# Weight sums placed behind the feed-forward's splits, k and v loads behind the sums: an attention and feed-forward kernel

## Chip, cores and metric

One core of one Trainium2 chip. The metric is device microseconds of one execution; the time of a kernel is the median of its runs.

## What is computed

For each batch b and head h, k and v are averaged over groups of 8 of their 576 positions, the softmax of q against the 72 pooled keys weighs the 72 pooled values, and the result, 4608 rows of 512, goes through a feed-forward with a leaky relu:

```python
k_p = k.reshape(B, H, Sp, pool, D).mean(axis=3)
v_p = v.reshape(B, H, Sp, pool, D).mean(axis=3)
scores = scale * np.matmul(q, k_p.transpose(0, 1, 3, 2))
...
out = np.matmul(attn, v_p)
...
h = x @ w_in                  # 4608x512 @ 512x2048
g = np.maximum(0.01 * h, h)
return g @ w_out              # 4608x2048 @ 2048x512
```

q, k and v have the shape 8 x 8 x 576 x 64, all float32.

## The kernel before

Every large product is made of three fp32r matmuls: an operand is split into a high part (a cast) and a low part (operand less high part), and high x high, high x low and low x high are added in PSUM.

**The feed-forward** goes in runs over chunks of 512 rows (`CH`). The list `runs` numbers them from 0: runs 0 to 4 share chunks 0 and 1 with the start, runs 5 to 9 take chunks 2 to 6 in full, runs 10 and 11 the last two chunks. In runs 5 to 9 a run has 16 steps f. In step f, `m1` makes a 128 x 512 block of x @ w_in in the PSUM tile `ph` (twelve matmuls, L1141 to L1143); ACT applies Prelu in place (L1146) and casts `gh` (L1149), DVE subtracts `gl` (L1150). `m2`, two steps behind, multiplies `gh` and `gl` with w_out into four accumulators `acc` (twelve matmuls, L1327 to L1329). There are two `ph` buffers, so the m1 of step f+2 waits for the `gl` of step f. The last step of a run stores the four accumulators (L1363 ff.): half copied by ACT, half by DVE into a tile `o`, then a store on SP's queue.

**Runs 10 and 11** take the weight blocks in eight pairs (`PAIRS`) and multiply by sums and differences of a pair's four halves, so that a pair needs fewer matmuls (`pair`, L1233 ff.). These are made beforehand: `prepare(j)` (L1171 ff.) adds the high and low parts of two weight blocks on DVE (L1180), forms four sums and differences (L1182 to L1186), casts the two results to `wsumh` on ACT (L1189), subtracts on DVE (L1190) and stores them in DRAM (`kept`, four stores on SP, L1200). For the first four pairs (`OPEN`) a fifth store keeps the half A22 of the weights as it is. The work of `prepare` is cut in eight pieces and two pairs (`EACH`) belong to each of runs 5 to 8.

**The attention** of batches 2 to 7 runs beside these runs, in units that the loop at L1488 ff. hands out between the pieces of m1 and m2: `lk` and `lv` load and pool k and v of a batch (loads L287, L304, L317; adds on POOL L264 and L271), `ku` and `vu` form kT and the value tiles `v_hi`, `v_lo`, `v_rem` (`v_parts`, L521, is the scaled remainder of v), `qT` is q transposed (L564), then for each tile t of 128 rows and each half g of the heads `pss` (scores, L599), `e` and `red` (softmax, L607 to L640), `at` (scaled weights, POOL, L643 and L649), `rows` (a store of `at` to DRAM, L660), `blocks` (loaded back in another order, L669), `pp` (transposed by DVE, L680), `pT` (its split, L702 to L709) and `pa` (weights x values on PE, L724 to L727), whose result, split again, is x of the feed-forward.

**Buffers.** One tag, `raw`, with two buffers in turn, holds the parts of k and v as loaded (k0raw, k1raw, kremraw, v0raw, v1raw, vremraw of a batch, in this order) and the weight sums (`wsum`, `wsumh`). Whoever takes a buffer waits until all readers of what was in it are done. Outputs `o` have a tag of their own with three buffers.

**What sets the order.** PE's order is that of the program. The other engines' are set by a list scheduler, which places an instruction by its program position and by what it expects of the engines; each engine and each DMA queue then runs its list strictly in turn. `tc.issue_after(x)` puts the instructions under it behind x. In the program the pieces of `prepare` are spread over the first half of a run:

```python
while n > REST and formed < min(1, 2 * beat / beats) * PIECES_OF * EACH:
    formed += 1
    next(forming, None)
```

(a run has 64 beats), and `lk`, `lv` of the next batch are put in the middle of the run's units (L1498 to L1500).

Of the kernel before, what the change touches and what calls it, by code (L numbers as in the profile page):

```python
# [24 lines left out]
def tile_pooled_attention_ffn(  # L25
# [9 lines left out]
    nc = tc.nc  # L35
# [463 lines left out]
    def place_v(b, sums, rem):  # L499
        if b < 2:  # L500
            pvm = bank(b, f"pvm{b}").rearrange("a p x -> a (p x)")[:, : NK * D]
            for g, half in enumerate(sums):
                for i in range(2):
                    nc.tensor.matmul(
                        pvm[:, 2 * g * D : 2 * (g + 1) * D],
                        addup[:, 1 - i : 3 - i, :].rearrange("r i s -> r (i s)"),
                        half[:, i::2, :], start=i == 0, stop=i == 1,
                    )
            sums = pvm.rearrange("a (p d) -> a p d", p=NK)
        for i in range(2):  # L510
            r = slice(64 * i, 64 * i + 64)
            pin(nc.scalar.mul(v_hi[r, :, i, :], sums[r], 1.0 / POOL))
        for i in range(2):
            r = slice(64 * i, 64 * i + 64)
            pin(nc.vector.scalar_tensor_tensor(
                v_lo[r, :, i, :], sums[r], 1.0 / POOL, v_hi[r, :, i, :].bitcast(F32),
                op0=ALU.mult, op1=ALU.subtract,
            ))
        if b > 1:
            yield  # L520
            pin(nc.scalar.mul(v_parts, rem, 1.0 / POOL))  # L521
            yield
            pin(nc.vector.scalar_tensor_tensor(
                rem, rem, 1.0 / POOL, v_parts.bitcast(F32), op0=ALU.mult, op1=ALU.subtract
            ))
            nc.vector.tensor_scalar(rem, rem, signs[:, 1:2], None, op0=ALU.mult)
            nc.vector.scalar_tensor_tensor(
                rem, v_parts.bitcast(F32), signs[:, 0:1], rem, op0=ALU.mult, op1=ALU.add
            )
            nc.vector.tensor_tensor(  # L530
                v_rem, rem.unsqueeze(2).broadcast_to([P, 2, 4, D]),
                heads.unsqueeze(1).unsqueeze(3).broadcast_to([P, 2, 4, D]), op=ALU.mult,
            )
            return
        for g in range(2):
            r, lo = slice(32 * g, 32 * g + 32), slice(64 + 32 * g, 96 + 32 * g)
            nc.scalar.mul(v_parts[r, g], rem[r, 0], 1.0 / POOL)
            nc.vector.scalar_tensor_tensor(
                v_parts[lo, g], rem[r, 0], 1.0 / POOL, v_parts[r, g].bitcast(F32),
                op0=ALU.mult, op1=ALU.subtract,  # L540
            )
        pv = bank(b, f"pv{b}").rearrange("a p x -> a (p x)")[:, : 2 * D]
        nc.tensor.matmul(
            pv, spread, v_parts.rearrange("s g d -> s (g d)"), start=True, stop=True
        )
        nc.vector.tensor_tensor(
            v_rem, pv.rearrange("s (g d) -> s g d", g=2).unsqueeze(2).broadcast_to([P, 2, 4, D]),
            heads.unsqueeze(1).unsqueeze(3).broadcast_to([P, 2, 4, D]), op=ALU.mult,
        )
# [574 lines left out]
    parts = [(n, c, f) for n, (c, fs, _) in enumerate(runs) for f in fs]  # L1124
    partial = dram.tile([CH, DM], F32, name="partial")
    back = []
    gs, accs = {}, {}

    def m1(k):

        n, c, f = parts[k]
        xh, xl = x_parts(c)
        w = ws[0, f]
        ts = runs[n][2]
        r = slice(ts[0] * P, (ts[-1] + 1) * P)
        w_ = len(ts) * P
        nm = f"{n}_{f}"
        ph = ps_h.tile([P, CH], F32, tag="h", name=f"ph{nm}")[:, :w_]
        for kk in range(NK):
            ks = slice(kk * P, (kk + 1) * P)  # L1140
            nc.tensor.matmul(ph, w[:, 0, ks], xh[kk][:, r], start=kk == 0, stop=False)  # L1141
            nc.tensor.matmul(ph, w[:, 0, ks], xl[kk][:, r], start=False, stop=False)  # L1142
            nc.tensor.matmul(ph, w[:, 1, ks], xh[kk][:, r], start=False, stop=kk == NK - 1)  # L1143
            if kk == 1:
                yield
        nc.scalar.activation(ph, ph, AF.Prelu, alpha=0.01)  # L1146
        gh = three.tile([P, CH], F32R, tag="gh", name=f"gh{nm}")[:, :w_]
        gl = three.tile([P, CH], F32R, tag="gl", name=f"gl{nm}")[:, :w_]
        casts.append(nc.scalar.copy(gh, ph))  # L1149
        nc.vector.tensor_tensor(gl, ph, gh.bitcast(F32), op=ALU.subtract)  # L1150
        gs[k] = gh, gl
        yield

# [16 lines left out]
    def prepare(j):  # L1170

        f0, f1 = PAIRS[j]
        raw = two.tile([P, 2, DM], F32, tag="raw", name=f"wsum{j}")
        w = [raw[:, k, :] for k in range(2)]
        raw = two.tile([P, 2, DM], F32R, tag="raw", name=f"wsumh{j}")
        h = [raw[:, k, :] for k in range(2)]
        (a11, a12), (a21, a22) = ((x[:, :HALF], x[:, HALF:]) for x in w)
        for x, f in zip(w, (f0, f1)):
            whole = ws[0, f].bitcast(F32)
            nc.vector.tensor_tensor(x, whole[:, 0, :], whole[:, 1, :], op=ALU.add)  # L1180
            yield
        nc.vector.tensor_tensor(a22, a21, a22, op=ALU.add)  # L1182
        nc.vector.tensor_tensor(a21, a11, a21, op=ALU.subtract)
        yield
        nc.vector.tensor_tensor(a11, a22, a11, op=ALU.subtract)
        nc.vector.tensor_tensor(a12, a12, a11, op=ALU.subtract)  # L1186
        yield
        for x, y in zip(w, h):
            nc.scalar.copy(y, x)  # L1189
            nc.vector.tensor_tensor(x.bitcast(F32R), x, y.bitcast(F32), op=ALU.subtract)  # L1190
            yield
        ship = [
            (kept[j, :, 2 - 2 * i : 4 - 2 * i, k, :], part.rearrange("p (s x) -> p s x", s=2))
            for i in range(2) for k, part in enumerate((h[i].bitcast(F32), w[i]))
        ]
        if j < OPEN:
            ship.append((kept[j, :, 4], ws[0, f1].bitcast(F32)[:, :, HALF:]))
        yield
        for to, of in ship:
            nc.sync.dma_start(to, of)  # L1200
        yield

    seats = {}
# [139 lines left out]
    def store(n, c, t, a):  # L1343
        end = n == len(runs) - 1
        if end and t == NT - 1:

            r = 2 * S - 2 * TAIL + (c - 2) * CH + t * P
            for i, copy in enumerate((nc.scalar.copy, nc.vector.tensor_copy)):
                cols = slice(i * DM // 2, (i + 1) * DM // 2)
                o = two.tile([P, DM // 2], F32, tag="raw", name=f"o{n}_{t}{i}")  # L1350
                copy(o, a[:, cols])
                (nc.scalar if i == 0 else nc.sync).dma_start(out[r : r + P, cols], o)
            return

        pool, tag = (two, "raw") if n == REST - 1 and t > 1 else (five, "o")
        o = pool.tile([P, DM], F32, tag=tag, name=f"o{n}_{t}")
        if end:
            if t % 2:
                nc.scalar.copy(o, a)
            else:  # L1360
                nc.vector.tensor_copy(o, a)
        elif n == REST:
            nc.vector.tensor_tensor(o, a, back[t], op=ALU.add)  # L1363
        else:
            nc.scalar.copy(o[:, : DM // 2], a[:, : DM // 2])
            nc.vector.tensor_copy(o[:, DM // 2 :], a[:, DM // 2 :])
        if n == 0:
            nc.sync.dma_start(partial[t * P : (t + 1) * P, :], o)
        elif c < 2:
            nc.sync.dma_start(out[c * S + t * P : c * S + (t + 1) * P, :], o)  # L1370
        elif c == 2 and t == 0:
            for b in range(2):
                nc.sync.dma_start(out[b * S + CH : (b + 1) * S, :], o[TAIL * b : TAIL * (b + 1), :])
        else:
            r = 2 * S - 2 * TAIL + (c - 2) * CH + t * P
            nc.sync.dma_start(out[r : r + P, :], o)


    steps = []
# [100 lines left out]

    PIECES_OF = 8
    EACH = -(-len(PAIRS) // (FAST - 3))

    def sums_of(js):
        for j in js:
# [4 lines left out]
    for n, (c, fs, ts) in enumerate(runs[: REST + FAST - 1]):  # L1490
# [3 lines left out]
        if n >= REST:  # L1494
            nxt = n - REST + 2
            if nxt in waiting:
                us.insert(0, lambda nxt=nxt: carry(nxt))
            mid = len(us) // 2  # L1498
            for b in early[n]:
                us[mid:mid] = [att[b]["lk"], att[b]["lv"]]  # L1500
            if n == REST:
# [5 lines left out]
        for f in fs:  # L1507
# [23 lines left out]
            for slot in slots:  # L1531
                for _ in slot:
                    beat += 1
                    while done < min(len(us), len(us) * beat // (beats - behind)):
                        us[done]()
                        done += 1
                    while n > REST and formed < min(1, 2 * beat / beats) * PIECES_OF * EACH:
                        formed += 1
                        next(forming, None)
            at += 1  # L1540
        while done < len(us):
            us[done]()
# [80 lines left out]
```

## Time and profile before

| what | value |
|---|---|
| median of 3 runs | 923.64 us (922.68 to 926.41) |
| the profiled execution | 926.44 us |
| its span in the trace | 924.7 us |
| PE, DVE, ACT, POOL busy | 890.6, 499.3, 433.4, 211.2 us |
| mean granted clock of PE | 0.987 of full speed |
| HBM read, written | 76.94 MB, 30.54 MB |

The profiled execution lies 1.7 us over its own span and 2.8 us over the median of the runs. Times in the rows are counted from the start of the span. An engine's idle time is only named with the instruction that ended it and the releaser, in brackets.

### The profile page before, as it was taken

What the parts mean: (1) busy time and instruction counts of PE and PEld (TensorE: products, weight loads), DVE (VectorE), ACT (ScalarE), POOL (GpSimd) and SP (SyncE); (2) the same over time, 40 slices, a digit from 0 to 9 for tenths busy, and PEclk for the clock granted to TensorE, in tenths of its full rate; (3) what the DMA queues carried; (4) which work ended last, traced back from release to release, by engine and by line L of the source; (5) the groups of instructions that cost most, each with busy time, mean ns of one, the idle gap of its engine ahead of it and who ended that gap; (6) DMA issues with size and microseconds to landing.
All of it is one profiled execution on the core that took longest, in us unless ns stands there. A gap on an engine that the chain in (4) does not pass through costs nothing.

```text
span 924.7 us, 13658 instructions
## 1 busy us (share of the span) xinstructions
PE 890.6 (96%) x4587; PEld 761.1 (82%) x4587; DVE 499.3 (54%) x1178; ACT 433.4 (47%) x1354; POOL 211.2 (23%) x388
## 2 busy tenths in 40 slices
PE   4599999999999989999999999999999999999998
PEld 4478888788888868888888878888888889989997
DVE  6999569545384572636555555553455442452222
ACT  5788558344344443533444345342544344453332
POOL 4511110343423312411232122411210321010000
PEclk9799999999999989999999999999999999999999
DMA  9985231427346453423534343620532055414342
GB/s 259 303 262 166 66 72 46 97 58 188 111 130 171 107 162 86 113 47 120 154 82 96 87 137 102 138 62 25 148 81 63 0 164 160 122 47 137 105 135 80
DMA packets 153029, 108.37 MB, mean 117 GB/s; under 512 B 99840, under 2 KB 133376, under 8 KB 152960
## 3 DMA queue, kind: packets, MB, share of 16 engines
q1 hardware_dynamic: 144976, 90.86, 36.4%
q10 hardware_dynamic: 7984, 16.65, 6.4%
q8 instruction: 36, 0.59, 0.3%
q14 instruction: 33, 0.27, 0.1%
HBM read 76.94 MB, written 30.54 MB: 116 GB/s over the span
## 4 chain that ended last, share of the span: by engine, by line
PE 80%; DVE 7%; DMA 5%; POOL 2%; SPq 2%; ACT 2%; issue 1%; POOLq 0%; ACTq 0%; DVEq 0%
PE acc L1327 12%; PE acc L1328 12%; PE acc L1329 12%; PE ph L1141 9%; PE ph L1143 9%; PE ph L1142 9%; PE ends_y L1233 5%; PE ends_x L1233 3%; PE pss L599 3%; DMA q<-in_q_dram 1%; DMA blocks<-rows 1%; PE pa L725 1%; PE pa L727 1%; PE pa L726 1%; PE pa L724 1%
## 5 line engine op out<-in xcount | busy, mean ns | idle before, releaser
L1327 PE MATMUL acc<-w,gh 128*128 128x512 f32 x576 | 227.6, 395 | 0.0
L1328 PE MATMUL acc<-w,gh 128*128 128x512 f32 x576 | 225.2, 391 | 0.0
L1329 PE MATMUL acc<-w,gl 128*128 128x512 f32 x576 | 224.5, 390 | 0.0
L1141 PE MATMUL ph<-xh,w 128*128 128x512 f32 (+1 forms) x480 | 185.4, 386 | 3.6 <-DVE gl L1150 3.6
L1142 PE MATMUL ph<-xl,w 128*128 128x512 f32 (+1 forms) x480 | 181.9, 379 | 0.0
L1143 PE MATMUL ph<-xh,w 128*128 128x512 f32 (+1 forms) x480 | 181.9, 379 | 0.0
L1329 PEld LDWEIGHTS acc<-w,gl 128*128 128x128 f32 x576 | 108.2, 188 | 23.4
L1146 ACT ACTIVATE ph<-ph 128x512 f32<-128x512 f32 (+1 forms) x120 | 67.1, 559 | 127.0 <-PE ph L1143 126.3
L609 ACT ACTIVATE e<-pss,red 128x72 f32<-128x72 f32 (+1 forms) x320 | 97.6, 328 | 57.5 <-DVE red L607 57.2
L1327 PEld LDWEIGHTS acc<-w,gh 128*128 128x128 f32 x576 | 108.5, 188 | 19.2
L1328 PEld LDWEIGHTS acc<-w,gh 128*128 128x128 f32 x576 | 108.5, 188 | 18.6
L1150 DVE TENSOR_TENSOR gl<-ph,gh 128x512 fp32r<-128x512 f32 (+1 forms) x120 | 77.6, 648 | 74.7 <-ACT gh L1149 73.7
L1141 PEld LDWEIGHTS ph<-xh,w 128*128 128x128 f32 x480 | 91.5, 191 | 19.8 <-DVE gl L1150 4.2
L1143 PEld LDWEIGHTS ph<-xh,w 128*128 128x128 f32 x480 | 91.3, 190 | 16.9
L1142 PEld LDWEIGHTS ph<-xl,w 128*128 128x128 f32 x480 | 91.4, 190 | 15.4
L643 POOL TENSOR_TENSOR at<-e,red 128x128 f32<-128x128 f32 (+1 forms) x120 | 48.4, 423 | 193.1 <-DVE red L640 116.1
L1149 ACT CAST gh<-ph 128x512 fp32r<-128x512 f32 (+1 forms) x120 | 67.1, 559 | 3.1
L609 ACT ACTIVATION_READ_ACCUMULATOR e<-pss,red 128x1 f32 (+1 forms) x320 | 68.4, 214 | 0.0
L607 DVE TENSOR_REDUCE red<-pss 128x4 f32<-128x288 f32 (+1 forms) x80 | 35.9, 453 | 55.8 <-PE pss L599 53.1
L680 DVE STREAM_TRANSPOSE pp<-blocks 128x384 f32<-128x384 f32 (+1 forms) x60 | 44.4, 760 | 38.6 <-DMA blocks<-rows 38.5
L702 ACT CAST pT_hi<-pp 128x384 fp32r<-128x384 f32 (+1 forms) x80 | 36.4, 479 | 45.9 <-DVE pp L680 42.6
L599 PE MATMUL pss<-kT,qT 128*128 128x144 f32 x320 | 48.8, 294 | 3.8 <-DVE qT L564 1.1
(244 smaller groups left out, 1263.5 us busy)
## 6 DMA issues: line engine op xcount, KB each, us to landing
seat<-kept ACTq DMA_DIRECT2D x21, 512.0 KB
rows<-at SPq DMA_DIRECT2D x48, 192.0 KB
blocks<-rows SPq DMA_DIRECT2D x48, 192.0 KB
out_dram<-o SPq DMA_DIRECT2D x34, 256.0 KB
w_bits<-in_moe_w_in_dram SPq DMA_DIRECT2D x16, 512.0 KB
w_bits<-in_moe_w_out_dram SPq DMA_DIRECT2D x16, 512.0 KB
q<-in_q_dram SPq DMA_DIRECT2D x96, 64.0 KB
kept<-wsumh SPq DMA_DIRECT2D x16, 256.0 KB
```

The source lines that it names most:

```text
L599: nc.tensor.matmul(sc[:, 2 * SP * i : 2 * SP * (i + 1)], qT[:, p, :], kT[:, p, :, :].rearrange("d i s -> d (i s)"), start=True, stop=True,)
L609: ins = nc.scalar.activation(e[:n, h, :], scv[:n, h, :], AF.Exp, bias=mx[:n, h : h + 1], accum_out=sm[:n, h : h + 1],)
L1141: nc.tensor.matmul(ph, w[:, 0, ks], xh[kk][:, r], start=kk == 0, stop=False)
L1142: nc.tensor.matmul(ph, w[:, 0, ks], xl[kk][:, r], start=False, stop=False)
L1143: nc.tensor.matmul(ph, w[:, 1, ks], xh[kk][:, r], start=False, stop=kk == NK - 1)
L1146: nc.scalar.activation(ph, ph, AF.Prelu, alpha=0.01)
L1149: casts.append(nc.scalar.copy(gh, ph))
L1150: nc.vector.tensor_tensor(gl, ph, gh.bitcast(F32), op=ALU.subtract)
L1233: nc.tensor.matmul(out, w[:, stay, ks], move, start=start and i + n == 0, stop=i + n == 3, skip_group_check=True,)
L1327: nc.tensor.matmul(a, gh[:, r], hi, start=first, stop=False)
L1328: nc.tensor.matmul(a, gh[:, r], lo, start=False, stop=False)
L1329: nc.tensor.matmul(a, gl[:, r], hi, start=False, stop=last)
```

## The change

Five edits:

- Scaling `v_parts` on ACT is put behind the scaling of `v_hi`.
- The A22 stores (`kept[j, :, 4]`) are put behind the newest store of an output tile.
- The fourth output tile of run 9 takes a `raw` buffer instead of one of the output buffers.
- `lk` and `lv` come after two thirds of a run's units instead of a half, from run 5 on.
- The pieces of `prepare` are spread over beats 8 to 30 of the 64, and each is put behind the newest `gh` cast on ACT and the newest `gl` subtract on DVE.

```diff
-            pin(nc.scalar.mul(v_hi[r, :, i, :], sums[r], 1.0 / POOL))
+            ins = pin(nc.scalar.mul(v_hi[r, :, i, :], sums[r], 1.0 / POOL))
...
-            pin(nc.scalar.mul(v_parts, rem, 1.0 / POOL))
+            with tc.issue_after(ins.ins):
+                pin(nc.scalar.mul(v_parts, rem, 1.0 / POOL))
...
-    gs, accs = {}, {}
+    gs, accs, lows, sent = {}, {}, [], []
...
-        nc.vector.tensor_tensor(gl, ph, gh.bitcast(F32), op=ALU.subtract)
+        lows.append(nc.vector.tensor_tensor(gl, ph, gh.bitcast(F32), op=ALU.subtract))
...
-        if j < OPEN:
-            ship.append((kept[j, :, 4], ws[0, f1].bitcast(F32)[:, :, HALF:]))
         yield
         for to, of in ship:
             nc.sync.dma_start(to, of)
+        if j < OPEN:
+            with tc.issue_after(sent[-1].ins):
+                nc.sync.dma_start(kept[j, :, 4], ws[0, f1].bitcast(F32)[:, :, HALF:])
         yield
...
-        pool, tag = (two, "raw") if n == REST - 1 and t > 1 else (five, "o")
+        apart = n == REST - 1 and t > 1 or n == REST + FAST - 2 and t == NT - 1
+        pool, tag = (two, "raw") if apart else (five, "o")
...
-            nc.sync.dma_start(out[r : r + P, :], o)
+            sent.append(nc.sync.dma_start(out[r : r + P, :], o))
...
+    FROM, UNTIL = 8, 30
...
-            mid = len(us) // 2
+            mid = len(us) * 2 // 3 if n > REST else len(us) // 2
...
-                    while n > REST and formed < min(1, 2 * beat / beats) * PIECES_OF * EACH:
+                    while n > REST and formed < min(1, (beat - FROM) / (UNTIL - FROM)) * PIECES_OF * EACH:
                         formed += 1
-                        next(forming, None)
+                        with tc.issue_after(casts[-1].ins), tc.issue_after(lows[-1].ins):
+                            next(forming, None)
```

Below are engines' lists at three places, as the scheduler leaves them. In a name like `gl_10_4381` the first number is the step (for attention tiles the tile and the half), the last a serial number; line numbers of the changed kernel differ by one from before's in these places.

**SP, run 5, around the loads of k.** Before:

```order
L1200 DMA kept<-wsumh_3072 128x2x256
L1200 DMA kept<-wsum_3071 128x2x256
L460 DMA q_4_3362<-in_q_dram 32x16x32 x2
L660 DMA rows_0_1_3174<-at_0_1_3170 128x4x96
L669 DMA blocks_3_1_3225<-rows_3_1_2910 128x384
L669 DMA blocks_4_1_3239<-rows_4_1_3015 128x192
L287 DMA k0raw_3258<-in_k_dram 64x2x512 x2
L287 DMA k1raw_3264<-in_k_dram 64x2x512 x2
```

Now:

```order
L1199 DMA kept<-wsum_3109 128x2x256
L1199 DMA kept<-wsumh_3110 128x2x256
L1199 DMA kept<-wsum_3109 128x2x256
L287 DMA k0raw_3402<-in_k_dram 64x2x512 x2
L287 DMA k1raw_3408<-in_k_dram 64x2x512 x2
L460 DMA q_0_3748<-in_q_dram 32x16x32 x4
L304 DMA kremraw_3415<-in_k_dram 64x1x512
L661 DMA rows_1_0_3315<-at_1_0_3311 128x4x96
```

Before, k0raw stands behind block loads, four places after the run's early sum stores (two more pairs' sums follow late in the same run). Now the four stores of the run's second sum, of which three are shown, stand right in front of it.

**ACT, run 5, around the Prelu of step 11** (`ph_11`). Before:

```order
L609 ACTIVATE e_2_1_3479,red_2_1_3480<-pss_2_1_3476,red_2_1_3480 64x72 x4
L1189 CAST wsumh_3741<-wsum_3740 128x512 x2
L521 ACTIVATE v_parts<-vremsum_3296 128x128
L1146 ACTIVATE ph_11_3506<-ph_11_3506 128x512
L702 CAST pT_hi<-pp_0_0_3553 128x3x128
L1149 CAST gh_11_3520<-ph_11_3506 128x512
```

Now:

```order
L610 ACTIVATE e_2_0_3469,red_2_0_3470<-pss_2_0_3466,red_2_0_3470 64x72 x4
L610 ACTIVATE e_2_1_3479,red_2_1_3480<-pss_2_1_3476,red_2_1_3480 64x72 x4
L1147 ACTIVATE ph_11_3506<-ph_11_3506 128x512
L703 CAST pT_hi<-pp_0_0_3553 128x3x128
L1150 CAST gh_11_3520<-ph_11_3506 128x512
L703 CAST pT_hi<-pp_1_0_3571 128x3x128
```

The two casts `wsumh` of the third pair, whose buffer is the one of this batch's `vremraw`, and the scaling `v_parts` stood ahead of the Prelu; the casts are now in run 6, and the Prelu follows the exponentials.

**DVE, run 6, around the subtract of step 10** (`gl_10`). Before:

```order
L530 TENSOR_TENSOR v_rem<-vremsum_3296,heads 128x512
L744 TENSOR_TENSOR xl_2_4271<-pa_1_2_4384,xh_2_4267 128x256
L1150 TENSOR_TENSOR gl_10_4381<-ph_10_4366,gh_10_4380 128x512
L515 SCALAR_TENSOR_TENSOR v_lo<-vsum_3295,v_hi 64x4x64
L680 STREAM_TRANSPOSE pp_0_0_4477<-blocks_0_0_4475 128x4x96
L515 SCALAR_TENSOR_TENSOR v_lo<-vsum_3295,v_hi 64x4x64
L744 TENSOR_TENSOR xl_3_4272<-pa_1_3_4391,xh_3_4268 128x256
L705 TENSOR_TENSOR pT_lo<-pp_0_0_4477,pT_hi 128x2x128
L709 SCALAR_TENSOR_TENSOR pT_hi<-pp_0_0_4477,marks,pT_hi 128x128
L680 STREAM_TRANSPOSE pp_1_0_4490<-blocks_1_0_4488 128x4x96
```

Now:

```order
L1151 TENSOR_TENSOR gl_9_4304<-ph_9_4281,gh_9_4303 128x512
L681 STREAM_TRANSPOSE pp_0_0_4477<-blocks_0_0_4475 128x4x96
L681 STREAM_TRANSPOSE pp_1_0_4490<-blocks_1_0_4488 128x4x96
L745 TENSOR_TENSOR xl_2_4200<-pa_1_2_4384,xh_2_4196 128x256
L681 STREAM_TRANSPOSE pp_0_1_4547<-blocks_0_1_4545 128x4x96
L1151 TENSOR_TENSOR gl_10_4381<-ph_10_4366,gh_10_4380 128x512
L515 SCALAR_TENSOR_TENSOR v_lo<-vsum_3429,v_hi 64x4x64 x2
```

Before, `gl_10` stands ahead of all three block transposes of the coming batch's first tiles; now `pp_0_0`, `pp_1_0` and `pp_0_1` stand ahead of it. The loads of that batch's k and v, before at the end of run 5, are now in run 6.

## Rows read from the trace of the kernel before

**Rows 1.** The page, part 1: busy us, share of the span, instructions.

```profile
PE 890.6 (96%) x4587; PEld 761.1 (82%) x4587; DVE 499.3 (54%) x1178; ACT 433.4 (47%) x1354; POOL 211.2 (23%) x388
```

**Rows 2.** PE's waits from 100 us on: us in total, times, longest.

```profile
PE ph L1141 <- DVE gl L1150: 3.2, 1, 3.2
PE pa L725 <- DVE pT_lo L705: 1.6, 1, 1.6
PE pss L599 <- DVE qT L564: 1.1, 1, 1.1
```

**Rows 3.** Windows of 5 us: length, busy per engine, granted clock (PEclk), DMA share, GB/s.

```profile
330.00:335.00 5.00, 3.65 (x9) 2.87 (x10) 4.28 (x12) 2.08 (x5) 0.00 (x0) 0.51 0.96 279
...
535.00:540.00 5.00, 3.42 (x17) 2.63 (x16) 4.95 (x16) 3.02 (x8) 0.00 (x0) 1.00 0.57 197
```

**Rows 4.** Timeline, PE, run 5: start, us, instruction, in brackets the idle time before.

```profile
331.36 0.79 PE L1141 MATMUL ph<-xh,w 128*128 128x512 f32 x1 [3.21 <-DVE gl L1150]
...
336.64 0.47 PE L724 MATMUL pa<-pT_hi,v_hi 128*128 128x320 f32 x1
```

**Rows 5.** Timeline, ACT, run 5.

```profile
327.51 1.14 ACT L1189 CAST wsumh<-wsum 128x512 fp32r<-128x512 f32 x2 [7.34 <-POOL vremsum L271]
...
328.77 0.57 ACT L1146 ACTIVATE ph<-ph 128x512 f32<-128x512 f32 x1
```

**Rows 6.** Timeline, DVE, run 5.

```profile
290.67 0.65 DVE L1150 TENSOR_TENSOR gl<-ph,gh 128x512 fp32r<-128x512 f32 x1
...
330.62 0.68 DVE L1150 TENSOR_TENSOR gl<-ph,gh 128x512 fp32r<-128x512 f32 x1
...
331.89 0.89 DVE L680 STREAM_TRANSPOSE pp<-blocks 128x384 f32<-128x384 f32 x1 [0.33 <-DMA blocks<-rows]
```

**Rows 7.** Timeline, SP, run 5: DMA issues.

```profile
288.02 1.32 SPq L287 DMA_DIRECT2D k0raw<-in_k_dram  x2
...
298.26 1.27 SPq L287 DMA_DIRECT2D v0raw<-in_v_dram  x2
...
313.95 5.38 SPq L317 DMA_DIRECT2D vremraw<-in_v_dram  x8
...
341.25 0.43 SPq L1200 DMA_DIRECT2D kept<-wsum  x1
...
343.22 1.33 SPq L287 DMA_DIRECT2D k0raw<-in_k_dram  x2
```

**Rows 8.** Timeline, POOL, run 5.

```profile
303.08 2.11 POOL L264 TENSOR_TENSOR v0raw<-v0raw 128x512 f32<-128x512 f32 x2 [0.17 <-DMA v0raw<-in_v_dram]
...
323.89 2.10 POOL L264 TENSOR_TENSOR vremraw<-vremraw 128x512 f32<-128x512 f32 x2 [9.84 <-DMA blocks<-rows]
...
325.95 0.75 POOL L643 TENSOR_TENSOR at<-e,red 64x128 f32<-64x128 f32 x2
```

**Rows 9.** Timeline, run 6: POOL, DVE, then PE twice.

```profile
388.80 2.12 POOL L264 TENSOR_TENSOR v1raw<-v1raw 128x512 f32<-128x512 f32 x2 [0.38 <-DMA v1raw<-in_v_dram]
...
398.29 1.26 DVE L1150 TENSOR_TENSOR gl<-ph,gh 128x512 fp32r<-128x512 f32 x2
...
424.07 0.39 PE L1141 MATMUL ph<-xh,w 128*128 128x512 f32 x1
...
426.79 0.39 PE L1327 MATMUL acc<-w,gh 128*128 128x512 f32 x1
```

**Rows 10.** Timeline, DVE, run 7.

```profile
537.41 1.28 DVE L1180 TENSOR_TENSOR wsum<-w 128x512 f32<-128x512 f32 x2
...
538.61 0.42 DVE L705 TENSOR_TENSOR pT_lo<-pp,pT_hi 128x256 fp32r<-128x256 f32 x1
```

**Rows 11.** Timeline, run 10: ACT, then DVE.

```profile
754.35 0.37 ACT L1365 COPY o<-acc 128x256 f32<-128x256 f32 x1 [1.33 <-DMA out_dram<-o]
...
755.10 1.07 DVE L564 STREAM_TRANSPOSE qT<-q 128x512 f32<-128x512 f32 x1
```

**Rows 12.** Window of 20 us at the start, columns as in rows 3.

```profile
40.00:60.00 20.00, 17.89 (x77) 14.18 (x77) 19.05 (x46) 17.55 (x50) 4.08 (x7) 0.74 0.93 309
```

More of the change, by code (lines that the diff above doesn't have):

```diff
@@ L1369, in store @@
         elif c < 2:
-            nc.sync.dma_start(out[c * S + t * P : c * S + (t + 1) * P, :], o)
+            sent.append(nc.sync.dma_start(out[c * S + t * P : c * S + (t + 1) * P, :], o))
         elif c == 2 and t == 0:
```

## The prediction

> **What bounds the kernel now.** I read the page first, then PE's waits, then the timelines around each wait. The page has PE busy 96% of the span [rows 1], so an edit off PE is worth only the PE idle that it removes or makes, plus what the clock does after it. From 100 us on PE waits long at three places that the edit touches [rows 2]: 3.2 us for a `gl` subtract, 1.6 us for a `pT_lo`, 1.1 us for a `qT`.
>
> The first costs more than itself. Idle ended at 331.36 after 3.21 us [rows 4]; in the stretch from 330 to 335 the granted clock was 0.51, so near the 1.2 GHz level, while from 535 to 540, with the 1.6 us wait in it, it stayed 1.00 [rows 3]. The twelve matmuls of m1 that follow took from 331.36 to 336.64, 5.28 us [rows 4]; the same twelve at full clock take 426.79 - 424.07 = 2.72 us [rows 9]. So this wait costs 3.2 + 2.6 = **5.8 us**. Its cause is on ACT: the casts `wsumh` of a weight sum stood idle for 7.34 us until 327.51, because the raw buffer was still with the batch's last v load (`vremraw`), and the feed-forward's Prelu, queued behind on ACT, came at 328.77 [rows 5], so `gl` only at 330.62 [rows 6].
>
> **The change, part by part.** The sum is made against the profiled execution, 926.4 us, which is 2.8 above the median of the runs, 923.6; I take 2.8 off at the end. About 0.5% (4.6 us) is what a measurement can tell from no change.
>
> *Sums in the first 40% of their run.* No cast waits for a v load any more, and Prelu is no longer behind one: **-5.8** in run 5. The same jam in run 7 delayed the `pT_lo` of 538.61 behind two sums of 1.28 us at 537.41 [rows 10]: **-1.6**, or nothing if another link is late there. The sums themselves add no instruction. On DVE and ACT they now lie beside m1 and m2 of steps 2 to 7. From the end of an m1 to the m1 two steps on, which needs its `gl`, PE has an m2, an m1 and an m2, twelve matmuls each, 3 x 2.72 = 8.2 us [rows 9]; Prelu, cast and subtract take about 0.6 + 0.6 + 0.7 [rows 5, 6], so a `gl` has some 6 us of slack, and the sums cost nothing unless something else queued with them is late.
>
> *Loads behind the sums, run 5.* k0raw now stands on SP behind the four `kept` stores of the second sum, and needs its raw buffer from them. In the trace the next load was issued 343.22 - 341.25 = 2.0 us after the start of such a last store [rows 7]. The second cast's subtract stands behind the `gl` of step 6, which ends at 291.3 [rows 6]; with 0.7 for the subtract, 0.4 for the store before, and 2.0, k0raw goes at 294.4 at the earliest, at 297 if the sums push that `gl` by 2.6. I take 295.5, between them, against 288.02 now [rows 7]: +7.5. What follows is tighter than before, since v's first sum on POOL is no longer behind the softmax tiles: 10.2 to the v0 issue as now (298.26 - 288.02 [rows 7]), 1.2 for a softmax tile newly ahead, 4.8 to the first add (303.08 - 298.26), 2.1 + 0.5 for pooling [rows 7, 8]. The eight v remainder loads then go 18.8 after k0raw, at 314.3 against 313.95, and land at 324.3 against 323.89 [rows 8] (the row names another transfer as what ended the wait, but the add reads the v remainder). Softmax tile 2 now stands behind one of the two remainder adds instead of both (2.10 together), so it starts about 325.5 against 325.95. From there to the first `pa` matmul it took 336.64 - 325.95 = 10.7 [rows 4, 8], part of it PE's own slowness; I take 1.0 off: 335.2. With no `gl` wait PE would reach that matmul at 331.36 - 3.21 + 2.72 = 330.9. So a wait of 4.3 takes the old one's place and, being longer than the 3.2 that halved the clock, I charge 2.6 again: **+6.9** (ends +3.2 for the earliest issue with the clock kept, +8.4 for the latest). Run 5 so comes out at +1.1.
>
> *Loads behind the sums, run 6.* In before these were issued at 343.22, before run 6 began; now in it. On DVE three block transposes now stand ahead of the `gl` of step 10, which was ahead of them. Call the issue of k0raw T. By the rows of run 5, v0raw's first add ends at T + 10.2 + 4.8 + 1.4; from a softmax tile on POOL to its block's transpose it took 331.89 - 325.95 = 5.9 [rows 6, 8]; with 0.7 for v0's other add and 2.3 for the transposes and the subtract, that `gl` ends at T + 25.3. PE needs it at 424.07 [rows 9]: T over 398.8 makes a wait. The `gl` of step 6, behind which the last sum's subtract and stores come, starts at 398.29 [rows 9]; with 0.6, 0.7, 0.4 and 2.0 as in run 5 that gives 402; but there the softmax waited on POOL behind a v load's adds until 390.9 [rows 9], and these are no longer ahead, which can bring T down to 398. Two sums' DVE work in that stretch speaks for later, 404.5. I take 399.8, nearest to the row that shows the cover gone: **+1.0** (ends 0 and +8.3).
>
> *Runs 7 and 8* have the same order without the transposes before the `gl` that decides; no row shows a lack there: 0 (ends 0 and +2). *The units moved two places earlier* change no matmul's count; cover is m1 and m2: 0. *v's scaling behind v_hi* removes an ACT idle that PE does not see: 0.
>
> *A22 copies out of the start.* Four stores of 256 KB go from the first 60 us to runs 5 and 6, where SP has room: 0 there. At the start DVE was busy 19.05 of 20 us while the DMA engines were 0.93 busy at 309 GB/s [rows 12]: 1 MB is 3.4 us of DMA time, but DVE is the bound; **-0.3** (ends 0 and -3.4). The Trainium skill, page "DMA: Bandwidth & Descriptors", section "Issuing engines are not separate DMA queues", says that all queues' transfers interleave on the same 16 engines, so the weight loads would gain what the copies took: by it alone this term would be -3.4. The trace agrees that the engines are full, but not that PE waits for them.
>
> *o3 in a raw buffer.* ACT's copy at 754.35 waited 1.33 for an output store, and `qT` on DVE came behind it at 755.10 [rows 11]; PE's wait for it was 1.1. It can fall to nothing, or q's own load ends last; **-0.7**, ends 0 and -1.1.
>
> Sum: -5.8 + 6.9 + 1.0 - 1.6 - 0.3 - 0.7 = -0.5, so 925.9, and 2.8 off: **923.1 us**, a swap of one wait for another. With its own ends this case holds 919 to 927.
>
> **The rivals.**
> *A, the waits go and none replaces them.* It needs `pa` in run 5 2.7 us sooner (a wait of 1.6 or less leaves the clock alone [rows 3]) and T under 399 in run 6. For it: half of the chain from softmax to `pa` ran beside jammed ACT and DVE work that is no longer there. Against: the v remainder's landing takes 9.9 us from first issue [rows 7, 8] in any order. Time: -5.8 + (0 to 1.6) - 1.6 - 0.3 - 0.7 = -8.4 to -6.8, so 915.2 to 916.8.
> *B, slower: the `gl` of run 6 behind the block transposes.* Place: DVE, step 10. It decides from T = 398.8, and from about 402 the wait is 3.2 and the clock halves. Price 3.2 + 2.6 = 5.8 at T = 402, 8.3 at 404.5. With the other terms (-1.5) that is +4.3 to +6.8: 927.9 to 930.4. For it: the rows that give 402. Against: the POOL adds that leave the stretch. The Trainium skill, "DMA: Bandwidth & Descriptors", "Rules for kernel authors", asks that a transfer be issued early and waited for late; this edit issues run 6's loads some 56 us later than before, and by that rule B is the outcome. The trace agrees in that the load issued at 343.22 was never waited for by PE.
> *C, the new wait of run 5 is short enough to keep the clock, and run 6 is clean:* that lies between A and the forecast, 917 to 919.
>
> **How the numbers follow.** Forecast 0.41, A 0.26, C 0.09, B 0.24. A and C are faster by over 0.5% (0.35), B is slower by over it nearly always (0.24), the forecast is within it (0.41). Leaving out some of A's and B's outer halves, 8 in 10 lies from 914.5 to 930.5.
>
> **What would show it.** Right: no `gl` wait near 331, k0raw of run 5 at about 295, a `pa` wait of some 4 us near 335 with a clock near 0.5 behind it, none over 1.5 us in run 6, no `pT_lo` wait near 538. A is shown by PE's waits after 100 us adding to under 3 us. B is shown by a wait for `gl` about 424 with transposes just ahead of it on DVE. I would be wrong in kind if the start, before 100 us, moved by over 1 us, or if run 7 or 8, which I cost at nothing, had a wait of their own.

## The result, and the profile after

| | before | changed |
|---|---|---|
| median of 6 runs | 924.58 us (922.68 to 926.41) | 932.70 us (929.27 to 933.40) |
| the profiled execution, its span | 926.44, 924.7 us | 933.40, 931.6 us |
| PE busy | 890.6 us | 894.1 us |

The ratio is 1.0084 [1.0064, 1.0104]: slower by 0.8%, above the range that was given. Rival B came true in run 6, and run 5 kept a wait of the old kind. Each kernel's profiled execution is the slowest of its six. PE's waits from 100 us on in the changed kernel (total, times, longest), beside [rows 2]:

```profile
PE ph L1142 <- DVE gl L1151: 7.6, 2, 4.7
PE pss L600 <- DVE kT L488: 1.1, 1, 1.1
PE pa L725 <- ACT pT_hi L703: 0.9, 1, 0.9
PE pa L726 <- DVE pT_lo L706: 0.9, 1, 0.9
```

The waits for `pT_lo` in run 7 and for `qT` in run 10 are gone, as foretold. But there are two long `gl` waits where there was one. Timeline of PE, and windows of 5 us (columns as in rows 3), beside [rows 3, 4]:

```profile
331.42 0.79 PE L1142 MATMUL ph<-xh,w 128*128 128x512 f32 x1 [2.95 <-DVE gl L1151]
...
336.80 0.42 PE L725 MATMUL pa<-pT_hi,v_hi 128*128 128x320 f32 x1 [0.92 <-ACT pT_hi L703]
338.12 0.64 PE L726 MATMUL pa<-pT_lo,v_hi 128*128 128x320 f32 x1 [0.90 <-DVE pT_lo L706]
...
432.01 0.80 PE L1142 MATMUL ph<-xh,w 128*128 128x512 f32 x1 [4.66 <-DVE gl L1151]
```

```profile
330.00:335.00 5.00, 3.58 (x9) 2.86 (x10) 1.37 (x3) 0.07 (x1) 2.15 (x5) 0.66 0.47 111
335.00:340.00 5.00, 3.18 (x12) 2.44 (x11) 4.38 (x11) 3.00 (x7) 0.00 (x0) 0.80 0.35 102
...
430.00:435.00 5.00, 2.99 (x7) 2.41 (x8) 4.78 (x14) 1.58 (x3) 1.23 (x2) 0.52 0.12 38
```

How far the same matmul lies behind its place in before tells where the time went. The first m1 matmuls of the steps are in step to within 0.4 us up to 331 us, but for two steps near 300 that the changed kernel makes good at once; there both kernels end a `gl` wait (331.36 and 331.42). One step later the changed kernel is 2.8 us behind (343.51 against 340.74), at the m1 that waits for `gl` of run 6's step 10 7.9 (432.01 against 424.07), one step on 10.4 (439.93 against 429.51). Of that, the waits of run 5 made 2.4 and those of run 6 7.4; another 0.7 came before them in two places without a long wait, 0.4 near 300 us and 0.3 near 370. Run 7 then gave back 1.9 and runs 10 and 11 1.6; the end of the span is 6.9 behind.

**Run 6: late loads, and a subtract in line behind them.** SP's issues, then POOL, DVE and ACT of the changed kernel:

```profile
403.63 0.36 SPq L1199 DMA_DIRECT2D kept<-wsum  x1
405.43 1.35 SPq L287 DMA_DIRECT2D k0raw<-in_k_dram  x2
...
415.53 1.27 SPq L287 DMA_DIRECT2D v0raw<-in_v_dram  x2
...
423.50 0.63 SPq L661 DMA_DIRECT2D rows<-at  x1
424.16 0.51 SPq L670 DMA_DIRECT2D blocks<-rows  x1
```

```profile
391.69 0.76 POOL L644 TENSOR_TENSOR at<-e,red 128x128 f32<-128x128 f32 x2 [6.80 <-ACT e L610]
...
420.48 1.29 POOL L264 TENSOR_TENSOR v0raw<-v0raw 128x512 f32<-128x512 f32 x1 [0.18 <-DMA v0raw<-in_v_dram]
421.73 0.76 POOL L644 TENSOR_TENSOR at<-e,red 128x128 f32<-128x128 f32 x2
```

```profile
387.98 1.29 DVE L1181 TENSOR_TENSOR wsum<-w 128x512 f32<-128x512 f32 x2 [2.83 <-DMA kept<-wsumh]
389.19 0.82 DVE L608 TENSOR_REDUCE red<-pss 128x4 f32<-128x288 f32 x2
...
402.93 0.68 DVE L1191 TENSOR_TENSOR wsum<-wsum,wsumh 128x512 fp32r<-128x512 f32 x1
...
427.15 0.86 DVE L681 STREAM_TRANSPOSE pp<-blocks 128x384 f32<-128x384 f32 x1 [6.95 <-DMA blocks<-rows]
429.31 0.86 DVE L681 STREAM_TRANSPOSE pp<-blocks 128x384 f32<-128x384 f32 x1 [1.31 <-DMA blocks<-rows]
430.02 0.40 DVE L745 TENSOR_TENSOR xl<-pa,xh 128x256 fp32r<-128x256 f32 x1
430.58 0.85 DVE L681 STREAM_TRANSPOSE pp<-blocks 128x384 f32<-128x384 f32 x1 [0.15 <-DMA blocks<-rows]
431.29 0.67 DVE L1151 TENSOR_TENSOR gl<-ph,gh 128x512 fp32r<-128x512 f32 x1
```

```profile
420.15 0.59 ACT L1150 CAST gh<-ph 128x512 fp32r<-128x512 f32 x1
```

The same `red` on DVE and the tile behind it on POOL, in before:

```profile
382.79 0.95 DVE L607 TENSOR_REDUCE red<-pss 128x4 f32<-128x288 f32 x2 [1.35 <-POOL k_rem L355]
```

```profile
390.87 0.94 POOL L643 TENSOR_TENSOR at<-e,red 128x128 f32<-128x128 f32 x2
```

The second `wsum` of the run could not begin before 387.98, when the stores of the first gave back the raw buffer; its last subtract ran at 402.93, its last store went at 403.63, and k0raw only then, at 405.43, against 343.22 before [rows 7]. The softmax stood behind that sum as well: `red` went on DVE at 389.19, 6.4 us later than in before with PE 3.0 behind, and its tile on POOL at 391.69, no sooner than in before (390.87), although no v load's adds were ahead of it any more. v0raw's first add came on POOL at 420.48 and the softmax tile `at_1_0` behind it at 421.73. On SP the store of that tile (`rows_1_0`, 423.50) stands behind the five k and v loads, and the first block load (`blocks_0_0`, 424.16) behind both, though the tile that it reads back had left POOL before 393. So the transpose, for which DVE had stood idle 6.95 us, came at 427.15. The cast `gh` of step 10 was over at 420.74, so that `gl` could have run 10 us sooner; it stood in DVE's list behind three transposes, and each waited for blocks.

**Run 5.** SP, DVE and ACT of the changed kernel:

```profile
296.46 1.32 SPq L287 DMA_DIRECT2D k0raw<-in_k_dram  x2
...
317.21 5.38 SPq L317 DMA_DIRECT2D vremraw<-in_v_dram  x8
322.70 1.98 SPq L460 DMA_DIRECT2D q<-in_q_dram  x3
324.73 0.62 SPq L670 DMA_DIRECT2D blocks<-rows  x1
```

```profile
328.17 0.86 DVE L681 STREAM_TRANSPOSE pp<-blocks 128x384 f32<-128x384 f32 x1 [9.43 <-DMA blocks<-rows]
...
330.69 0.68 DVE L1151 TENSOR_TENSOR gl<-ph,gh 128x512 fp32r<-128x512 f32 x1
```

```profile
329.07 0.51 ACT L703 CAST pT_hi<-pp 128x384 fp32r<-128x384 f32 x1 [8.13 <-DVE pp L681]
329.49 0.58 ACT L1150 CAST gh<-ph 128x512 fp32r<-128x512 f32 x1
```

k0raw went at 296.46 against 288.02 [rows 7]. The first block load stood on SP behind the eight vremraw loads and three q loads (324.73), so its transpose came at 328.17; on ACT the cast `pT_hi`, which needs that transpose, stood ahead of the cast `gh`, on DVE the transpose stood ahead of `gl`: 330.69, the same time as before (330.62 [rows 6]) for another reason.

### The profile page after: what moved, and what is told of

Same layout as the page of the kernel before. It is cut to its first block, busy times and chain, and to the rows that moved or that the text cites. A ratio compares the mean times of both kernels' runs of the same rounds, so it can differ in the third digit from the quotient of the medians.

```text
span 931.6 us, 13681 instructions
## 1 busy us (share of the span) xinstructions
PE 894.1 (96%) x4587; PEld 762.7 (82%) x4587; DVE 505.9 (54%) x1178; ACT 434.3 (47%) x1354; POOL 218.7 (23%) x388
## 4 chain that ended last, share of the span: by engine, by line
PE 56%; DMA 5%; POOL 2%; DVE 2%; SPq 1%; ACT 1%; issue 1%; POOLq 0%; DVEq 0%; ACTq 0%
PE acc L1329 9%; PE acc L1330 9%; PE acc L1331 9%; PE ph L1142 6%; PE ph L1143 6%; PE ph L1144 6%; PE ends_y L1235 5%; PE ends_x L1235 4%; PE pss L600 2%; DMA blocks<-rows 1%; DMA kept<-wsumh 1%; PE pa L726 1%; POOL at L644 1%; DMA k1raw<-in_k_dram 1%; PE pa L728 1%
## 5 line engine op out<-in xcount | busy, mean ns | idle before, releaser
L644 POOL TENSOR_TENSOR at<-e,red 128x128 f32<-128x128 f32 (+1 forms) x120 | 52.6, 458 | 223.2 <-DVE red L641 111.1
```

## The experiments

The theory: the whole loss lies in the sums' place, which makes the k and v loads late; lateness costs PE only through the lists in which a `gl` or `gh` stands behind work that needs those loads. One rival is that another of the five edits loses; another that lateness alone costs, wherever the subtract stands. Every ratio is to before, run on the same chip beside the experiment.

**1, 2. The sums alone, and all but the sums.** First, before with this edit alone (and the list `lows` that it needs):

```diff
+    FROM, UNTIL = 8, 30
...
-                    while n > REST and formed < min(1, 2 * beat / beats) * PIECES_OF * EACH:
+                    while n > REST and formed < min(1, (beat - FROM) / (UNTIL - FROM)) * PIECES_OF * EACH:
                         formed += 1
-                        next(forming, None)
+                        with tc.issue_after(casts[-1].ins), tc.issue_after(lows[-1].ins):
+                            next(forming, None)
```

> The kernel before with the sums' new place alone (beats 8 to 30, behind the newest cast and subtract); units, A22 stores, v's scaling and run 9's output as before. Theory (the loss comes from the k and v loads that now wait for the sums' stores, and from two feed-forward subtracts, run 5 step 11 and run 6 step 10, that stand behind late attention work): the whole loss is here, 931 to 934, with waits for gl of 2.5 to 3.5 us near 331 and 4 to 5 us near 432, and the wait of about 1 us for qT in run 10 still there. Rival (the units' new place and the other edits cost the time, the sums nothing): 923 to 925.

Second, the changed kernel with just this edit taken back:

```diff
-                    while n > REST and formed < min(1, (beat - FROM) / (UNTIL - FROM)) * PIECES_OF * EACH:
+                    while n > REST and formed < min(1, 2 * beat / beats) * PIECES_OF * EACH:
                         formed += 1
-                        with tc.issue_after(casts[-1].ins), tc.issue_after(lows[-1].ins):
-                            next(forming, None)
+                        next(forming, None)
```

> The changed kernel with the sums spread over the first half again and not queued; the other four edits stay. Theory: no loss, 922 to 925, k0raw of run 6 issued before run 6 begins, no wait for gl near 432. Rival (units and other edits cost): 931 to 933.

Measured: the sums alone 1.0111 [1.0088, 1.0133] (932.5 us), k0raw at 296.15 and 401.45, `gl` waits of 2.90 and 2.40 at 332.99 and 433.31, the second shorter than foretold, and 1.1 for a `qT` still there. All but the sums 1.0024 [1.0013, 1.0035] (925.2 us), k0raw at 288.90 and 343.16, a `gl` wait of 2.10 near 331, none in run 6 and none for `qT`. So the loss is in the sums' place; the other four edits together cost 0.2%, though the `qT` wait goes with them.

**3. Transposes and `pT_hi` behind the newest step.** All block transposes behind the newest `gl`, the `pT_hi` cast behind the newest `gh`:

```diff
+        with nullcontext() if pinned else tc.issue_after(lows[-1].ins):
             pin(nc.vector.transpose(
...
+        with tc.issue_after(casts[-1].ins) if b >= VIA and not pinned else nullcontext():
             ins = nc.scalar.copy(pc["hi"][:, :, o : o + n], pp[:, 0:3, :n])
```

> The changed kernel with each block transpose queued behind the newest gl and each pT cast behind the newest gh; nothing else moves by hand. Theory: in run 6 the subtract of step 10 no longer stands behind three transposes, its wait of 4.7 us and the halved clock after it (together 7.3) go, 925 to 926; in run 5 the wait changes from gl to pa and stays, 5 to 8 us in all. Rival (the sums' own work in steps 2 to 7 makes the splits late, whatever stands around them): 932 to 933 with the same gl wait near 432.

Measured: 1.0090 [1.0075, 1.0105] (930.8 us). All `gl` waits are gone though k0raw went at 404.08 in run 6, but five waits of PE for `pT_hi`, 5.7 us in all and 3.3 the longest, came in their place. Four of these, of 0.6 us each near 245, 401, 543 and 641 us, lie outside the two stretches, and by the step offsets against the changed kernel some 1.2 us was lost at each. Holding back every transpose is too much; the two places need a narrower edit.

**4, 5. The v remainder as a unit of its own, then with a hold in the second half of a run.**

```diff
-            if b > 1:
-                raws.append(load_v_rem(b))
-            if b > 1:
-                pooled(eng, rem, raws[2], P)
...
+        def rest():
+            raws.append(load_v_rem(b))
+            pooled(eng, rem, raws[2], P)
...
+                if n > REST:
+                    us.append(att[b]["lr"])
```

> The changed kernel with a batch's v remainder (eight loads on SP, two adds and a sum on POOL) made a unit of its own at the end of the run instead of behind the v loads. Theory: in run 5 blocks of tile 0 and the softmax of tile 2 no longer stand behind it, the waits near 331 to 338 go (8.2 us with the clock), run 6's wait stays: 924 to 926. Rival (run 5 waits for the k and v loads' lateness as such, through ksum on ACT or POOL's adds): the wait near 331 stays at 2 us or more, 930 to 933.

The next kernel adds to this, from run 6 on and from step 9 of a run:

```diff
+            held = n > REST + 1 and f >= 9
...
+        with tc.issue_after(lows[-1].ins) if held and not pinned else nullcontext():
             pin(nc.vector.transpose(
```

> The v remainder as a unit at the end of the run (as in the run before this) and, from run 6 on and from step 9 of a run, each block transpose queued behind the newest gl. Theory (two separate orders cost the time): run 5's wait and run 6's wait are both gone, 8 us each with the clock, the time falls to 915 to 919 against 924 for the kernel before. Rival (the lateness of the k and v loads itself costs, whatever is ordered behind them): with gl free, PE waits for pa instead in run 6 by 4 us or more, 922 to 928.

Measured: the unit alone 1.0115 [1.0094, 1.0137] (932.1 us). The edit did not do what it says: the scheduler listed the eight loads where they had been, and they went at 313.50. k0raw went earlier than in the changed kernel (293.69 and 397.77), yet the `gl` wait of run 6 grew to 6.66, because DVE's list there has twelve operations between the first transpose and `gl_10`, against three in the changed kernel. With the hold 0.9985 [0.9969, 1.0001] (922.7 us), k0raw at 294.27 and 399.02; run 5 kept a wait of 2.26, so the 915 to 919 that was expected is missed. PE's waits for a `gl`, with the hold missing, then with it:

```profile
PE ph L1149 <- DVE gl L1158: 9.7, 3, 6.7
```

```profile
PE ph L1151 <- DVE gl L1160: 2.3, 1, 2.3
```

DVE in run 6, from the first transpose to `gl_10` with the hold missing, then from `gl_10` to the first transpose with it:

```profile
419.67 0.87 DVE L681 STREAM_TRANSPOSE pp<-blocks 128x384 f32<-128x384 f32 x1 [7.16 <-DMA blocks<-rows]
...
426.93 0.69 DVE L1158 TENSOR_TENSOR gl<-ph,gh 128x512 fp32r<-128x512 f32 x1
```

```profile
418.75 0.68 DVE L1160 TENSOR_TENSOR gl<-ph,gh 128x512 fp32r<-128x512 f32 x1
...
421.72 0.85 DVE L683 STREAM_TRANSPOSE pp<-blocks 128x384 f32<-128x384 f32 x1
```

The loads are as late in both, 1.3 us later even with the hold: from k0raw's issue to the time at which PE is ready for the m1 that needs `gl_10` it is 23 us in either (22 in the changed kernel; the hold on that kernel as it stands was not run). In the list with the hold `gl_10` and `gl_11` stand ahead of the first transpose. Order alone is worth 9.4 us by the medians. So lateness by itself, as far as it goes here, does not cost: that rival falls.

**6. The same unit in before.** The diff is that of experiment 4.

> The kernel before, only the v remainder made a unit of its own at the end of a run. Theory: the sums' casts of run 5 no longer wait for its buffer, and the chain to pa is shorter too, so the wait of 3.2 us and the clock after it (5.8) go without moving the sums: 917 to 919. Rival (without the sums' new place a cast still waits in front of a Prelu): a wait for gl near 331 or later stays, 923 to 925.

Measured: 1.0035 [1.0022, 1.0048] (928.0 us); vremraw at 314.18, so again not moved, and `gl` waits of 1.28, 2.88 and 0.31. Of its question this run tells nothing, and it is slower than both ranges; why is not known.

**7, 8. Sums earlier, and sums last.** First `FROM, UNTIL = 8, 30` becomes:

```diff
-    FROM, UNTIL = 8, 30
+    FROM, UNTIL = 0, 22
```

> The changed kernel with the sums in beats 0 to 22 instead of 8 to 30, queued as before this. Theory (what decides in run 6 is when k0raw is issued, with 398.8 as the point from which it costs): k0raw of run 6 goes some 6 to 10 us earlier and the wait of 4.7 for gl falls under 1 us; run 5's wait also falls by half or more: 921 to 926. Rival (order alone decides, not lateness): the wait for gl in run 6 stays at 4 us, 931 to 934.

Then the sums behind the loads, with the units back at a half and the unit of experiment 4:

```diff
-    FROM, UNTIL = 8, 30
+    FROM, UNTIL = 44, 64
...
-            mid = len(us) * 2 // 3 if n > REST else len(us) // 2
+            mid = len(us) // 2
```

> Sums in beats 44 to 64 of the run, queued behind the newest cast and subtract, so behind the batch's loads instead of ahead of them; units at a half; the v remainder at the end of the run. Theory: k0raw of run 5 and run 6 is as early as in the kernel before or earlier, no cast stands ahead of a Prelu, no wait of over 1.5 us from 250 to 640: 914 to 918. Rival (the sums late in a run jam the splits whatever they are queued behind): a wait for gl in steps 13 to 15 of a run or in the first of the next, 922 to 930.

Measured: earlier 0.9990 [0.9976, 1.0004] (923.2 us), k0raw at 289.18 and 381.64, no `gl` wait over 0.3. In this kernel's DVE list `gl_10` of run 6 stands behind the same three transposes, in the same order, as in the changed kernel; the loads go 24 us sooner, the transposes run from 411.33 on, `gl_10` is over at 416.42, 5 us before PE needs it, and the wait is gone. Last: 0.9963 [0.9946, 0.9979] (921.9 us), one wait of 1.8 for an output copy; slower than the 914 to 918 expected, and without the rival's waits.

So the wait of run 6 needs both: late loads with the transposes held cost nothing (5), the transposes ahead with early loads neither (7), the two together 4.66 us of idle and a halved clock.

**9, 10. The v remainder behind the block loads, then with the hold.** The loads of the remainder are now tied, so that they cannot move back:

```diff
-        nc.sync.dma_start(
+        fetched.append(nc.sync.dma_start(
             blocks[:, :m].rearrange("p a i j -> p (a i j)"),
...
+        def rest(behind):
+            with tc.issue_after(fetched[-1].ins) if behind else nullcontext():
+                raws.append(load_v_rem(b))
+            pooled(eng, rem, raws[2], P)
```

> The changed kernel, the v remainder's eight loads now ordered on SP behind the newest block load (in the runs before this that made it a late unit the scheduler put the loads back to where they were). Theory: in run 5 blocks of tile 0 no longer stand behind 5.4 us of issues nor the softmax of tile 2 behind the remainder's adds, so the waits from 331 to 338 (8.2 us with the clock) fall to under 2; run 6's wait for gl stays at 4 us or more: 924 to 927. Rival (only the 3 us by which k0raw came sooner helped there): run 5's wait stays at 2 us or more.

The hold is that of experiment 5.

> As the run before this, and the block transposes of run 6 on queued behind the newest gl from step 9. Theory: both waits gone, PE waits under 2 us in all from 280 to 450: 915 to 919. Rival: pa in run 6 becomes late, one wait of 3 us or more: 921 to 925.

Measured: without the hold 1.0053 [1.0038, 1.0068] (929.5 us). SP there has the blocks ahead, and PE stays busy in run 5 though k0raw went only at 295.19; windows and SP of this kernel:

```profile
322.44 4.38 SPq L671 DMA_DIRECT2D blocks<-rows  x5
326.87 5.38 SPq L317 DMA_DIRECT2D vremraw<-in_v_dram  x8
```

```profile
330.00:335.00 5.00, 5.00 (x26) 4.33 (x25) 3.41 (x10) 3.01 (x7) 0.00 (x0) 1.00 0.26 81
...
425.00:430.00 5.00, 3.53 (x8) 2.81 (x9) 3.61 (x9) 0.39 (x1) 0.00 (x0) 0.50 0.25 80
```

Run 6 still has its wait (6.52 us, ended at 426.47), longer than in the changed kernel, and run 7 one of 1.52, so the time is over the 924 to 927 expected. With the hold 0.9927 [0.9910, 0.9943] (917.8 us, 916.7 to 918.2): faster than both kernels. PE's waits from 100 us on, all of them, and two windows:

```profile
PE pss L602 <- DVE kT L490: 0.7, 1, 0.7
```

```profile
330.00:335.00 5.00, 5.00 (x24) 4.14 (x23) 3.28 (x9) 2.70 (x7) 0.79 (x1) 1.00 0.18 63
...
425.00:430.00 5.00, 5.00 (x25) 4.20 (x25) 2.72 (x5) 2.29 (x5) 2.50 (x3) 1.00 0.09 34
```

Here too the loads of run 6 are as late as without the hold, 23 us ahead of PE's need. The sums stand where the changed kernel has them, so their own work on DVE and ACT, the rival of experiment 3, does not make the splits late.

**11. The remainder behind the blocks, in before.** The diff of experiment 9, on before.

> The kernel before with the v remainder behind the newest block load, the sums where they were. Theory: its raw buffer comes after the sums' in turn, so the sums' casts wait for v1's and krem's buffers and not for the remainder; no wait for gl near 331: 917 to 920. Rival (a cast placed ahead of a Prelu waits for some buffer anyway): a gl wait of 2 us or more stays: 922 to 926.

Measured: 0.9966 [0.9955, 0.9977] (921.7 us), vremraw at 325.39, no wait near 331; 1.24 for a `gl` at 286.99 and 1.4 for a `qT` remain. Moving the 5.4 us of loads also helps the old order, but not by the link that was expected. The casts of the sums still waited for the remainder's buffer, only later, and behind the Prelu of step 11 (322.66) instead of ahead of it:

```profile
337.35 1.14 ACT L1197 CAST wsumh<-wsum 128x512 fp32r<-128x512 f32 x2 [3.92 <-POOL vremsum L271]
```

**12. Before once more,** unchanged, to see its wait in run 5 in a second execution.

> The kernel before, unchanged, once more with a profile. Its profiled execution was the slowest of its runs, 926.4 against a median of 923.8. Theory: the 3.2 us wait in run 5 lies at the edge at which the clock falls; in a faster execution it is under 3 us, the clock stays at 1.00 in 330 to 340, and the span is 921 to 923. Rival (the runs differ at the start, in the first 60 us): the wait and the clock near 331 read as before.

Measured: 921.9 us, one execution, 1.5 under the fastest of the ten beside it (923.4 to 926.3). PE's waits for the feed-forward and `pa`, and the window, against [rows 2, 3]:

```profile
PE ph L1141 <- DVE gl L1150: 1.3, 1, 1.3
PE pa L725 <- DVE pT_lo L705: 1.3, 2, 0.8
```

```profile
330.00:335.00 5.00, 4.54 (x23) 3.65 (x22) 4.62 (x10) 1.84 (x4) 0.00 (x0) 1.00 0.78 246
```

The wait that the prediction priced at 5.8 was here 1.3 with the clock whole: the same kernel has it in two sizes. From the m1 before the wait to the second behind it (steps 12 to 14 of run 5) it took 14.5 us here, 18.2 in the first execution and 12.1 in experiment 10, which has no wait there.

## Why the prediction was wrong

Term by term, the measured sizes taken from the step offsets of the two profiled executions:

| term | predicted | measured |
|---|---|---|
| run 5, old wait off, new wait on | -5.8 + 6.9 = +1.1 | +2.4 |
| run 6 | +1.0 | +7.4 |
| run 7, `pT_lo` | -1.6 | -1.9 |
| start | -0.3 | 0, within 0.3 |
| runs 10 and 11, `o3` and `qT` | -0.7 | -1.6 |
| runs 5 and 6, ahead of their waits | no term | +0.7 |
| profiled execution against median | -2.8 | before -1.9, changed -0.7 |

**Run 6 is the step that failed.** "I take 399.8, nearest to the row that shows the cover gone" should have been 405.4. Of the two ends, 398 and 404.5, the text held the softmax's release from POOL for decisive, and put the sums' own DVE work into the late end only. The trace shows a link that it lacked: the two sums of a run share the raw buffers, so the second starts when the stores of the first end (387.98 [2.83]), the softmax's `red` stands behind it on DVE (389.19), and so its tile started on POOL no sooner than in before (391.69 against 390.87). The `gl` of step 6, 398.29 in before, went at 402.34 and the sum's last subtract behind it, at 402.93. The chain from there was sized well: T + 25.3 gives 430.7 for the end of `gl`, measured 432.0. With T = 405.4, and PE 3.1 late by then, B's rule gives (405.4 - 398.8 - 3.1) + 2.6 = 6.1, measured 7.4; the missing 1.3 is that later `gl`. Mechanism, place and about the price of B were right; its chance, 0.24, hung on one badly chosen issue time. A and C, which both need run 6 clean, fell with it.

**Run 5: a new wait of about the foretold cost at about the foretold issue, but by another link.** Set beside experiment 10's, the stretch cost 8.5 us (20.6 - 12.1 for the same steps) where 6.9 was charged. k0raw was predicted at 295.5 and went at 296.46; vremraw 314.3 and 317.21, its add 324.3 and 327.34. The wait was expected on `pa`, with "no `gl` wait near 331". The lists shown ahead of the prediction had the cast `pT_hi` between `ph_11` and `gh_11`, before and now; I read there only that the `wsumh` casts left. With the transposes late, that cast kept `gh` and `gl` waiting, and 0.92 + 0.90 of the `pa` wait came on top, with the clock halved again behind them.

**The gain of -5.8 was that of one execution.** For the profiled one of before the size is right (18.2 - 12.1 = 6.1), but that of experiment 12 had 1.3 us of `gl` wait there and no clock loss. Of the 4.5 us between the two spans, 3.7 lie in this stretch and 0.8 at run 7's `pT_lo`, so that taking 2.8 off at the end counted part of the same losses twice; where a run at the median lies between the two is not known. In line with that, the median of the changed kernel lies 8.1 over that of before, while the profiled executions differ by 7.0.

**Right:** the `pT_lo` wait of run 7, the `qT` wait of run 10, no gain at the start, nothing lost in runs 7 and 8. That the sums' place alone took the `pT_lo` wait away is not shown: with the sums alone (experiment 1) run 7 has 1.0 us of waits for `pT`, with all but the sums 0.7, and experiment 12 has 0.8 in before itself. The start moved by less than 0.3 us. The copies did leave it: from 40 to 60 us the DMA share fell from 0.93 [rows 12] to 0.75, and PE was at most 0.2 us further at 100 us. So of the 3.4 that the Trainium skill's page "DMA: Bandwidth & Descriptors" ("Issuing engines are not separate DMA queues") would give, almost nothing came: the trace agrees that the copies took room on the 16 engines, but not that PE waited for it. The Trainium skill's advice on that page to issue a transfer early ("Rules for kernel authors") pointed to the right outcome here; experiments 5 and 10 bound it, as loads issued 51 to 56 us later than in before cost nothing once no `gl` stood behind them.

What stays open: which of the two sizes of before's wait in run 5 is the commoner, why experiment 6 is slower than before, and what makes the 0.7 us ahead of the waits.

## What to carry to other kernels

When a load is moved later, list for each engine what stands behind its consumers, down to the third or fourth link, and tie the work of the bounding engine ahead of them; that order was worth 9 to 12 us here, with the loads equally late. Where an edit queues a transfer behind other work, its issue time is the end of that work's whole chain of buffers, not of its last operation. And read a second execution's trace before pricing a wait that could as well have been short.

## What was not expected of the hardware

The prediction took a wait of 3.2 us as long enough to halve the clock and 1.6 as short enough not to. The length of the one wait does not decide it. Granted clock over 1 us after such waits, first in experiment 2 (wait of 2.10 us), then in experiment 1 (2.90 us), experiment 4 (2.43 us) and experiment 6 (2.88 us):

```profile
332.00:333.00 1.00, 1.00 (x4) 0.71 (x4) 1.00 (x2) 0.00 (x0) 0.00 (x0) 0.50 0.84 249
```

```profile
333.00:334.00 1.00, 1.00 (x4) 0.85 (x5) 0.00 (x0) 0.00 (x0) 0.00 (x0) 1.00 0.74 215
```

```profile
330.00:331.00 1.00, 1.00 (x5) 0.83 (x6) 1.00 (x5) 0.70 (x2) 0.00 (x0) 1.00 0.50 144
```

```profile
333.00:334.00 1.00, 1.00 (x4) 0.80 (x3) 1.00 (x5) 0.10 (x1) 0.00 (x0) 0.50 1.05 337
```

After 2.10 and 2.88 us the clock was at the 1.2 GHz level, after 2.43 and 2.90 at 2.4; in experiment 1 itself the shorter wait of 2.40, ended at 433.31, was followed by 0.50 from 434 to 435. In each case PE had been busy at full clock before the idle time. What the lower level cost varies too: from the m1 behind the wait to the next step's it took 8.3 us in experiment 6 and 9.4 in before, against 6.8 in experiment 4 and 6.7 in experiment 10, so 1.7 to 2.7 us. So whether a wait of 2 to 3 us costs its own length or that much more changed from one such place and execution to the next, and a price for it needs both values as ends of a range.
